# Multiplying the first MLP weight into attention's landmark values, batch by batch

## The chip, the cores and the metric

The kernel runs on one core of a Trainium2 chip. A core has TensorE (PE, matrix products), VectorE (DVE), ScalarE (ACT) and GpSimd (POOL), each with its own instruction stream that it executes in order, and SyncE (SP), whose queue starts most of the DMA transfers. The engines wait for each other by semaphores. Matrix products read SBUF and write PSUM. The metric is the device time of one execution in microseconds, as the median of several runs.

## The reference, cut to what matters

Nystrom attention over 8 batches of 8 heads, 576 rows of 64 elements each, with 32 landmarks a head, then a layer norm and a two-layer MLP with a residual:

```python
q_lm = q.reshape(B, H, 32, 18, D).mean(axis=3)      # landmarks; the same for k
A  = softmax(q @ k_lm.T / 8)                        # 576 x 32 for each head
Bm = softmax(q_lm @ k_lm.T / 8)                     # 32 x 32
C  = softmax(q_lm @ k.T / 8)                        # 32 x 576
Z  = Bm.T / (norm1(Bm) * norminf(Bm))
for _ in range(6):
    Z = 2 * Z - Z @ Bm @ Z
x  = A @ Z @ C @ v                                  # heads side by side: 576 x 512 a batch
xn = (x - mean(x)) / sqrt(var(x) + 1e-6) * g_ln
out = x + relu(xn @ w_ch1) @ w_ch2                  # 512 -> 2048 -> 512
```

For the change it matters that `x` of a batch is `A` (576 rows by 8 heads times 32 landmarks = 256) times `zc = Z C v`, and that the layer norm's division by a positive number a row can be done after the Relu and the second layer.

## The kernel before, in words

Work comes in units of four heads of one batch, two units a batch. Batches 0 and 1 go through `attention`, the others through `attention2` in the sets (2), (3, 4), (5, 6) and (7). For a set, a `Coming` object holds three queues of preparation: loads on SP's queue, casts to fp16 on POOL, and jobs. A job turns a tile with DVE's 32x32 transposes (`turn`), adds up segments of 18 rows for the landmarks (`add_up`; q's of most units are added on POOL), or spreads the sums with a small matmul into `psl` (`spread`), which ACT copies to `lm`. Then the set computes landmark scores (`psb`), scores of the landmarks of q with k (`psec`), the gram matrix (`psse`), the product with v (`pscv`), six iterations (`psn`), in which the scores of q with k's landmarks are done as well (`psea`, exponentiated into `ea`), and `zc` (`pszc`), spread by head masks into the block-diagonal tiles `zcbd`. `rows_of` then makes blocks of 128 rows of `x`: two matmuls of `ea` with `zcbd` into `psy`. The tiles `zcbd` have columns of head ones, so that `psy` also holds the softmax sums; DVE takes their reciprocals (`rcpd`) and multiplies, with a running row sum for the mean.

The MLP works on groups of 512 rows of `x`, nine in all, across batches. Each block is squared with an accumulator on ACT for the variance, centred (`center`, mostly on POOL) into `xn`, and turned by DMA (groups 0 and 1 by PE through `psxt`). The first layer contracts the 512 columns: for each of 16 chunks of 128 hidden columns, four matmuls of 512 columns into `psh`, which ACT passes through Relu to `hT`. The second layer is, in groups 0 to 3, 16 matmuls of 512 columns for each block into `pso`; in groups 4 to 8 it is a product of two-by-two blocks with seven products in place of eight (`pspa`, `pspe`, `pspc`, 256 columns a matmul), for which DVE adds and subtracts halves of `hT` (`hmix`) and POOL prepares mixes of `w2`. DVE or the additions of the products then form the output, which SP stores.

The order of the work is written out by hand. `mlp` is a generator of matmuls. `fill(n)` takes n pieces of it and is called between the steps of the attention, with counts that are listed for each set in `steps`; `prepare` casts, loads and runs jobs of the next set at the same places. All engines follow the program's order (`keep`). PSUM has three pools: `ps1` with one buffer, `ps2` with two (attention's larger tiles), and `psM` with three, for `psh`, `pso` and the product tiles. Nearly every instruction is issued by a helper, so in the profile matmuls have line L75, transposes by PE L79, and the ordered instructions of DVE, ACT and POOL L69; groups are told apart by their tiles' names.

Of the kernel before, what the change touches and what calls it, by code (L numbers as in the profile page):

```python
# [20 lines left out]
def kernel(  # L21
# [23 lines left out]
    G_FAST = 4  # L45
    HK, HN = MCH // 2, DM // 2
# [12 lines left out]
    nat = ctx.enter_context(tc.tile_pool(name="nat", bufs=8))  # L59
# [29 lines left out]
    raw = {0: {}, 1: {}}  # L89

    def load_qk(b):
        for u in range(U):
            raw[b]["q", u] = load(q, b, u, nc.sync)
            raw[b]["k", u] = load(k, b, u, nc.sync)

    def load_v(b):
        for u in range(U):
            raw[b]["v", u] = load(v, b, u, nc.sync)

# [7 lines left out]
    def cast_qk(b, u, nm, engine):  # L109
        t = nat.tile([P, NJ, 2, D], FP16, name="nat", tag="nat")  # L110
        engine.tensor_copy(out=t[:].rearrange("p j r d -> p r j d"), in_=raw[b][nm, u][:])
        nat_tiles[b, nm, u] = t

    def cast_v(b):
        natv_of[b] = natv = natv_buf[b % NV]
        for u in range(U):
            pool.tensor_copy(out=natv[:, u, :, :, 0:D].rearrange("p j r d -> p r j d"),
                             in_=raw[b]["v", u][:])

    nat_tiles, natv_of = {}, {}  # L120
    load_qk(0)
    load_v(0)
    g_sb = wpool.tile([P, KCH], FP32, name="g_sb")
    g_rows = wpool.tile([KCH, P], FP32, name="g_rows")
    keep(nc.sync.dma_start(out=g_rows[:], in_=moe_g_ln.rearrange("(c p) -> c p", p=P)))
# [11 lines left out]

# [6 lines left out]

# [13 lines left out]

# [16 lines left out]
    nc.vector.memset(eps_ln[:], 1e-6)  # L175

# [8 lines left out]
    zcbd_buf = []  # L185
    for i in range(NZ):
        zcbd_buf.append(const.tile([P, 4 * (D + 1)], FP16, name=f"zcbd{i}"))

    def zc_of(i):
        return zcbd_buf[i][:, ds(4 if i % 2 == 0 else 0, 4 * D)].rearrange("p (h d) -> p h d", d=D)

    cast_v(0)
    bones = const.tile([P, 4, 32], FP16, name="bones")
    for u in range(U):
        for nm in ("q", "k"):
            cast_qk(0, u, nm, dve)
        if u == 0:

            dve.tensor_copy(out=bones[:], in_=mask4[:, :, None].broadcast_to([P, 4, 32]))
            for i, t in enumerate(zcbd_buf):
                dve.tensor_copy(out=t[:, ds(0 if i % 2 == 0 else 4 * D, 4)],
                                in_=(mask4[:] if i < 2 else heads_of[i % 2]))


    load_qk(1)
    for u in range(U):
        for nm in ("q", "k"):
            cast_qk(1, u, nm, pool)  # L210
# [5 lines left out]
    xpool = ctx.enter_context(tc.tile_pool(name="xpool", bufs=15))  # L216

    def w_stage(src):
        stg = stage.tile([P, 2, DM], FP32, name="wstg", tag="stg")
        keep(nc.sync.dma_start(out=stg[:], in_=src))  # L220
        return stg

    def fetch_w1():
        coming = []
        for i in range(10):
            if i < 8:
                f, half = divmod(i, 2)
                coming.append(w_stage(w1_src[:, 2 * half:2 * half + 2, ts(f, DM)]))
            if i >= 2:
                f, half = divmod(i - 2, 2)  # L230
                stg = coming.pop(0)
                for c in range(2):
                    k = 2 * half + c
                    pool.tensor_scalar(out=w1_16[:, k, ts(f, DM)], in0=stg[:, c, :],
                                       scalar1=g_sb[:, k:k + 1], scalar2=0.0,
                                       op0=ALU.mult, op1=ALU.add)

    def fetch_w2():
        coming = []
        for i in range(12):  # L240
            if i < 8:
                coming.append(w_stage(w2_src[:, ts(i, 2), :]))
            if i >= 4:
                pool.tensor_copy(out=w2_16[:, ts(i - 4, 2), :], in_=coming.pop(0)[:])

    aprep = ctx.enter_context(tc.tile_pool(name="aprep", bufs=5))
    aexp = ctx.enter_context(tc.tile_pool(name="aexp", bufs=12))
    asm = ctx.enter_context(tc.tile_pool(name="asm", bufs=2))
    asum = ctx.enter_context(tc.tile_pool(name="asum", bufs=1))

    mstat = ctx.enter_context(tc.tile_pool(name="mstat", bufs=6))
    mxn = ctx.enter_context(tc.tile_pool(name="mxn", bufs=6))
    mxnT = ctx.enter_context(tc.tile_pool(name="mxnT", bufs=2))
    mhT = ctx.enter_context(tc.tile_pool(name="mhT", bufs=1))
    mout = ctx.enter_context(tc.tile_pool(name="mout", bufs=4))
# [4 lines left out]

# [13 lines left out]

    nat_pss, early_xT = {}, {}

    def sums(b, w, i, n16):
        for j in range(NJ):
            MM(nat_pss[b, i][:, w, :], n16[:, j, :, :].rearrange("p r d -> p (r d)"),
               pm16[:], start=(j == 0), stop=(j == NJ - 1), skip=True)  # L280

    def turn_part(w, nm, part):
        j0, j1 = ((0, 5), (5, NJ))[part]
        n16 = nat_tiles[1, nm, w]
        if part == 0:
            early_xT[1, nm, w] = aprep.tile([P, NJ, P], FP16, name="xT", tag="xT" + nm,
                                            bufs=5 if nm == "q" else 4)
        pst = psM.tile([P, 5, P], FP16, name="pst", tag="pm")
        for j in range(j0, j1):
            TR(pst[:, j - j0, :], n16[:, j, :, :].rearrange("p r d -> p (r d)"), ident16[:])  # L290
# [537 lines left out]
    def center(j, engine):  # L828
# [13 lines left out]
        if g < 2:  # L842
            return
# [435 lines left out]
```

The softmax here doesn't subtract the row's maximum and nothing guards it: scores larger than these inputs give would overflow.

## Time and profile before

| | us |
|---|---|
| time, median of three runs (lowest, highest) | 312.26 (311.87, 312.96) |
| span of the profiled execution, first to last instruction | 312.6 |
| PE busy | 303.4 |
| DVE busy | 191.6 |
| ACT busy | 155.6 |
| POOL busy | 140.7 |
| granted TensorE clock, mean | 0.989 |
| HBM read, written | 36.70 MB, 9.44 MB |

The profile is of one execution. It lists the busy time of each engine, the same in 40 equal slices of the span (a digit is tenths), groups of like instructions with their count, busy time and mean length, the idle time before them with what ended it, the chain of work that ended last, and the instructions in order of time. The profiler models the ends of matmuls, which are pipelined, so a busy PE need not be working at its full rate; how far apart matmuls start tells that.

### The profile page before, as it was taken

Reading aid. Unit: us, or ns where it says so; the run is one execution under the profiler, and the core shown is the slowest. Engines: PE = TensorE matmul, PEld = TensorE weight load, DVE = VectorE, ACT = ScalarE, POOL = GpSimd, SP = SyncE. Lnnn points to the kernel's source line nnn. Section 1 sums busy time; section 2 is a strip of 40 time slices with the busy share of each in tenths; the row PEclk is TensorE's granted clock in tenths of the full one; section 3 lists DMA queues with packets and bytes.
Section 4 is the critical chain, followed back from the end, with each engine's and each line's share of the span. In section 5 each row is a group of like instructions: output and inputs, shape, how many; then the busy total and the mean of one; then the engine's idle time right before and its main releaser. Section 6 shows DMA issues by size and latency. Waiting matters only on the chain.

```text
span 312.6 us, 8486 instructions
## 1 busy us (share of the span) xinstructions
PE 303.4 (97%) x3475; PEld 180.4 (58%) x3475; DVE 191.6 (61%) x525; ACT 155.6 (50%) x309; POOL 140.7 (45%) x191
## 2 busy tenths in 40 slices
PE   7899999999999999999999999999999999999994
PEld 7567764544444544544454468547844874685583
DVE  3648328957785326899256787749644980671364
ACT  2447783468524871277354761693147506405600
POOL 4479878974979595598097412030002240000000
PEclk9959999999999999999999999999999999999999
DMA  7999999999997877850159401540050516105013
GB/s 267 390 387 385 386 388 285 334 237 308 264 234 157 286 190 208 132 204 0 37 87 250 98 2 36 122 81 5 0 136 5 65 37 142 25 3 134 0 36 101
DMA packets 38863, 50.36 MB, mean 161 GB/s; under 512 B 17572, under 2 KB 18088, under 8 KB 38824
## 3 DMA queue, kind: packets, MB, share of 16 engines
q1 hardware_dynamic: 38504, 49.43, 56.4%
q8 instruction: 27, 0.44, 0.6%
q10 hardware_dynamic: 320, 0.39, 0.4%
q14 instruction: 12, 0.10, 0.1%
HBM read 36.70 MB, written 9.44 MB: 148 GB/s over the span
## 4 chain that ended last, share of the span: by engine, by line
PE 93%; DMA 2%; DVE 2%; issue 1%; SPq 0%; ACT 0%
PE psh L75 41%; PE pso L75 18%; PE pspa L75 8%; PE pspe L75 6%; PE pspc L75 6%; PE psy L75 3%; DMA stg<-in_k_dram 2%; PE psn L75 2%; PE pscv L75 2%; PE psec L75 1%; PE pst L79 1%; PE psea L75 1%; PE psse L75 1%; PE psa L75 1%; DVE xblk L69 1%; PE psxt L79 1%
## 5 line engine op out<-in xcount | busy, mean ns | idle before, releaser
L75 PE MATMUL psh<-xnT,w 128*128 128x512 f16 (+1 forms) x640 | 136.4, 359 | 0.7 <-issue 0.7
L69 ACT ACTIVATE hT<-psh 128x512 f16<-128x512 f32 x144 | 84.7, 598 | 71.8 <-PE psh L75 71.5
L75 PEld LDWEIGHTS <-w 128*128 128x128 f16 x640 | 58.8, 98 | 56.3 <-issue 4.8
L75 PEld LDWEIGHTS <-hT 128*128 128x128 f16 x656 | 62.8, 98 | 30.3 <-issue 1.1
L75 PE MATMUL pso<-w,hT 128*128 128x512 f16 x256 | 61.1, 380 | 0.0
L69 POOL TENSOR_SCALAR xn<-xblk,negm,rstd 128x512 f16<-128x512 f32 x20 | 16.8, 851 | 67.3 <-DVE negm L69 33.1
L69 ACT ACTIVATE junk<-xblk,negm 128x512 f16<-128x512 f32 x36 | 25.9, 720 | 18.9 <-POOL negm L69 11.6
L69 DVE SCALAR_TENSOR_TENSOR xblk<-psy,rcpd 128x512 f32<-128x512 f32 (+1 forms) x40 | 27.6, 691 | 1.8
L69 DVE SCALAR_TENSOR_TENSOR st<-st,psn 128x128 f16<-128x128 f16 (+2 forms) x36 | 11.4, 317 | 24.7 <-PE psn L75 24.3
L69 DVE TENSOR_TENSOR hmix<-hT 128x256 f16<-128x256 f16 (+2 forms) x20 | 8.9, 444 | 21.6 <-ACT hT L69 21.6
L69 POOL CAST nat<-stg 128x1152 f16<-128x1152 f32 x15 | 17.1, 1145 | 8.9 <-DMA stg<-in_q_dram 5.0
L69 DVE STREAM_TRANSPOSE xT<-nat 128x576 uint32<-128x576 uint32 x24 | 18.5, 769 | 0.0
L69 DVE TENSOR_REDUCE part<-xT 128x32 f16<-128x576 f16 x26 | 18.3, 744 | 0.1
L69 DVE RECIPROCAL rcpd<-psy 128x8 f32<-128x8 f32 (+1 forms) x40 | 8.1, 202 | 15.8 <-PE psy L75 15.5
L69 DVE SCALAR_TENSOR_TENSOR ot<-pso,rstd,xblk 128x512 f32<-128x512 f32 x16 | 12.0, 748 | 8.3 <-PE pso L75 8.3
L75 PEld LDWEIGHTS <-hmix 128*128 128x128 f16 x160 | 15.6, 98 | 1.9 <-issue 0.2
L69 DVE TENSOR_TENSOR xblk<-pspa,xblk 128x256 f32<-128x256 f32 x38 | 14.0, 418 | 4.2 <-PE pspa L75 4.2
L69 POOL CAST nat<-ring 128x1152 f16<-128x1152 f32 x12 | 13.6, 1144 | 6.7 <-DMA ring<-in_k_dram 3.3
L75 PE MATMUL psy<-zcbd,ea 128*128 128x260 f16 (+1 forms) x80 | 15.9, 284 | 0.0
L69 POOL CAST natv<-stg 128x1152 f16<-128x1152 f32 x10 | 11.4, 1161 | 7.6 <-DMA stg<-in_v_dram 7.6
L75 PEld LDWEIGHTS <-st 32*32 32x32 f16 x448 | 5.6, 90 | 14.8 <-issue 8.0
L69 POOL TENSOR_TENSOR asum<-asum 128x256 f32<-128x256 f32 (+1 forms) x22 | 13.1, 594 | 1.7
(130 smaller groups left out, 382.7 us busy)
## 6 DMA issues: line engine op xcount, KB each, us to landing
wstg<-in_moe_w_ch_dram SPq DMA_DIRECT2D x16, 512.0 KB, 7.0
stg<-in_q_dram SPq DMA_DIRECT2D x10, 576.0 KB, 7.8
stg<-in_k_dram SPq DMA_DIRECT2D x10, 576.0 KB, 7.6
out_dram<-xblk SPq DMA_DIRECT2D x34, 128.0 KB, 2.3
out_dram<-ot SPq DMA_DIRECT2D x32, 128.0 KB, 2.7
stg<-in_v_dram SPq DMA_DIRECT2D x7, 576.0 KB, 9.5
ring<-in_k_dram SPq DMA_DIRECT2D x6, 576.0 KB, 6.4
ring<-in_q_dram SPq DMA_DIRECT2D x6, 576.0 KB, 6.1
```

The lines of the kernel that those rows point to most:

```text
L69: return lambda *args, **kw: keep(getattr(self.engine, op)(*args, **kw))
L75: keep(nc.tensor.matmul(o, l, r, start=start, stop=stop, tile_position=(rb, cb), skip_group_check=(skip or cb != 0)))
L79: keep(nc.tensor.matmul(o, i_, idn, is_transpose=True, tile_position=(0, 0)))
```

## The change

The first layer no longer contracts the 512 columns of a turned `xn`. For each batch, `zc` (turned, `pszt`, copied to `zt`) is multiplied into `W1`: eight matmuls of 64 rows by 32 columns, 512 wide, make 256 landmark rows times 512 hidden columns (`product_of_heads`, `psm`, copied to `m16` by ACT or DVE), four such groups for the 2048 hidden columns. The first layer is then `m16` times `ea`, two matmuls of 288 columns for each half of the 576 rows. For this q's softmax must be normalized in `ea` itself (`normalize`: sums by a matmul, `1/s` as Exp of minus Ln on ACT, a product on DVE for batches 0 and 1, on POOL else). The row mean falls away because the columns of `W1` (scaled by `g`) are centred: `less_mean` sums them with a matmul, `center_w1` subtracts in place on DVE; batch 0's product uses the uncentred `W1` and is corrected in `m16` with `rz`. Mean and variance come from DVE's `bn_stats` and `bn_aggr`. `psy` has no columns of ones and is copied to `xblk` as it is. Every fourth `psh` tile goes through Relu on DVE.

The MLP goes batch by batch: blocks that straddle two batches belong to the odd batch, whose `hT` starts with the 64 last rows of the batch before (copied by POOL). `mlp` interleaves the second layer of a batch with the first layer of the next. The second layer has no seven-product form; for batch 0 it goes by halves of the columns, as `W2` is loaded by halves. Batch 1 is a set of its own through `attention2`, with its product with v late (`late`). `W1` and `W2` are loaded earlier on SP's queue: `W1` before batch 1's q and k, `W2` before batch 1's v. No `xn`, no transposing DMAs, no mixes of `w2` or `h` remain.

```diff
+    def normalize(ea, engine):
+        pss = ps2.tile([P, 2, 512], FP32, name="psd", tag="p2")
+        for half in range(2):
+            MM(pss[:, half, 0:HS], ones_of_heads, ea[:, ts(half, HS)])
+        lns = alog.tile([P, 2, HS], FP32, name="lns", tag="lns")
+        act(lns[:], pss[:, :, 0:HS], AF.Ln)
+        act(lns[:], lns[:], AF.Exp, scale=-1.0)
+        engine.tensor_tensor(out=ea, in0=ea, in1=lns[:].rearrange("p a t -> p (a t)"), op=ALU.mult)
...
-                dve.reciprocal(
...
-                    in1=rcpd[rows, :, None].broadcast_to([n, 8, D]),
-                    op0=ALU.mult, op1=ALU.mult, accum_out=rowsum[j][rows, :])
+                dve.tensor_copy(out=xb[rows, :], in_=psy[rows, :])
...
+        dve.bn_stats(out=six[:], in_=x_blk[j][:])
+        dve.bn_aggr(out=stats_of[b][:, u, :], in_=six[:])
...
+    def less_mean(f):
+        psf = psM.tile([P, 512], FP32, name="psf", tag="pm")
+        for c in range(KCH):
+            MM(psf[:], lesser[:], w1_16[:, c, ts(f, 512)], start=(c == 0), stop=(c == KCH - 1))
+        scalar.copy(less(f), psf[:])
+    def center_w1(f):
+        dve.tensor_tensor(out=w1_16[:, :, ts(f, 512)], in0=w1_16[:, :, ts(f, 512)],
+                          in1=less(f)[:, None, :].broadcast_to([P, KCH, 512]), op=ALU.add)
...
+        def product_of_heads(f):
+            psm = ps2.tile([P, 2, 512], FP32, name="psm", tag="p2")
+            for r in range(2):
+                for e in range(2):
+                    for u in range(U):
+                        block = 2 * r + e if b == 0 else 2 * (e ^ u) + r
+                        rows = ds(64 * e, 64)
+                        MM(psm[ds(32 * block, 32), u, :], zt[rows, r, w0 + u, :],
+                           w1_16[rows, 2 * u + r, ts(f, 512)], rb=64 * e, cb=32 * block)
...
+            elif f % 2 == 0:
+                scalar.copy(t[:], psm[:])
+            else:
+                dve.tensor_copy(out=t[:], in_=psm[:])
...
-                    psh = psM.tile([P, 512], FP32, name="psh", tag="pm")
-                    for c in range(KCH):
-                        MM(psh[:], w1_16[:, c, ts(m, P)], xnT[:, c, :],
-                           start=(c == 0), stop=(c == KCH - 1))
-                    act(hT[:, m, :], psh[:], AF.Relu)
+            for half in range(2):
+                psh = psM.tile([P, HS], FP32, name="psh", tag="pm")
+                for u in range(U):
+                    MM(psh[:], m16[f][:, u, ts(m % 4, P)], ea[u][:, ts(half, HS)],
+                       start=(u == 0), stop=(u == U - 1))
+                o = hT[:, m, ds(base + HS * half, HS)]
+                if n % 4 == 3:
+                    dve.tensor_scalar(out=o, in0=psh[:], scalar1=0.0, scalar2=None, op0=ALU.max)
+                else:
+                    act(o, psh[:], AF.Relu)
...
-                if g >= G_FAST:
-                    yield from second_layer(g, hT, mixed)
...
+        for b in range(B):
+            ahead, done, owed = None, False, 0
+            for cols in second_layer(b):
+                yield cols
+                if ahead is None and b + 1 in ready:
+                    ahead = first_layer(b + 1)
+                owed += cols
+                if ahead and not done and owed >= 1024:
+                    owed -= 1024
+                    cols = next(ahead, None)
...
+    for i in range(8):
+        load_w1(i)
...
+    for _ in range(4):
+        b1.next_load()
+        b1.next_cast()
+    for i in range(8):
+        load_w2(i)
+        cast_w2(i)
...
+    sets = [Coming((1,), 1), Coming((2,)), Coming((3, 4), 1), Coming((5, 6)), Coming((7,))]
```

`fill` now counts matmul columns (512 for each piece asked for) in place of pieces, `lesser` is a tile of -1/512, `less` holds the negated column means, `ones_of_heads` has a block of ones for each head, and `UP` is a factor of 16 in `g` that the variance's scale takes out again.

## The prediction

> **What bounds the kernel now.** I read the page's busy shares and slices first, then the chain of work that ended last, then the groups by form, the busy time by stretch, and one piece of the timeline.
>
> ```profile
> PE 303.4 (97%) x3475; PEld 180.4 (58%) x3475; DVE 191.6 (61%) x525; ACT 155.6 (50%) x309; POOL 140.7 (45%) x191
> ...
> PE   7899999999999999999999999999999999999994
> ...
> DVE  3648328957785326899256787749644980671364
> ...
> PE 93%; DMA 2%; DVE 2%; issue 1%; SPq 0%; ACT 0%
> ```
>
> TensorE is busy from the second slice to the last and makes 93% of the chain; DVE, next, is at 61%, with single slices at nine tenths. Whether a busy PE is also a dense one, the chain in order of time tells (start, length, what):
>
> ```profile
> 254.61 1.75 PE pspc L75 x16
> 256.36 13.81 PE psh L75 x64
> 270.17 1.75 PE pspa L75 x16
> ```
>
> 64 matmuls of 512 columns take 13.81 us, 0.2158 each; 16 of 256 take 1.75, 0.109 each, each with weights of its own. So a column costs 0.417 ns and a matmul 2.5 ns more: 288 columns are 0.1225 us. Most of the span is this dense. The number of columns decides today.
>
> ```profile
> 37.91 0.36 PE psa L75 x8
> ...
> 63.84 0.52 PE psec L75 x26
> ...
> 219.77 1.31 PE pspa L75 x12
> 221.23 0.36 PE psea L75 x29
> ```
>
> Small matmuls in different places of the array run at once: psec is 32 matmuls of 288 columns (26 recorded), 3.9 us in a row, and takes 0.52. Entering such a group costs something: twelve 256-column matmuls are 1.31 us here, and psea begins only 1.46 us after them. From start to start such a group costs about 0.09 us beside its own work.
>
> The durations of the other engines come from the groups by form (busy us, mean ns of one | idle before):
>
> ```profile
> L69 ACT ACTIVATE hT<-psh 128x512 f16<-128x512 f32 x144 | 84.7, 598 | 71.8 <-PE psh L75 71.5
> ...
> L69 ACT ACTIVATE junk<-xblk,negm 128x512 f16<-128x512 f32 x36 | 25.9, 720 | 18.9 <-POOL negm L69 11.6 <-DVE negm L69 7.1
> ...
> L69 DVE SCALAR_TENSOR_TENSOR xblk<-psy,rcpd 128x512 f32<-128x512 f32 x32 | 22.1, 692 | 1.5
> ...
> L69 DVE STREAM_TRANSPOSE xT<-nat 128x576 uint32<-128x576 uint32 x24 | 18.5, 769 | 0.0
> ...
> L69 DVE TENSOR_REDUCE part<-xT 128x32 f16<-128x576 f16 x26 | 18.3, 744 | 0.1
> ...
> L69 DVE TENSOR_TENSOR zcbd<-pszc,heads 128x256 f16<-128x256 f32 x12 | 4.3, 419 | 4.0 <-PE pszc L75 4.0
> ...
> L69 DVE TENSOR_TENSOR hT<-hT 128x1024 f16<-128x1024 f16 x10 | 7.2, 722 | 0.0
> ...
> L69 DVE CAST nat<-stg 128x1152 f16<-128x1152 f32 x4 | 3.0, 760 | 5.4 <-DMA stg<-in_q_dram 4.0 <-DMA stg<-in_k_dram 1.4
> ...
> L69 DVE TENSOR_SCALAR xn<-xblk,negm 128x512 f16<-128x512 f32 x2 | 1.6, 792 | 0.1
> ```
>
> A piece of the timeline (start, length), and one stretch of 18 us with each engine's busy time, PE, its weight loads, DVE, ACT, POOL:
>
> ```profile
> 137.54 0.77 DVE L69 STREAM_TRANSPOSE xT<-nat 128x576 uint32<-128x576 uint32 x1
> ...
> 138.23 0.20 DVE L69 STREAM_TRANSPOSE sT<-s 128x64 uint32<-128x64 uint32 x1
> ```
>
> ```profile
> 122.00:140.00 18.00, 18.00 (x92) 8.72 (x92) 15.88 (x43) 7.71 (x18) 11.91 (x18) 1.00 0.79 193
> ```
>
> The two transposes start 0.69 us apart though the first lasts 0.77: a DVE instruction whose operands are there occupies DVE for its mean less about 0.08 us. The stretch has DVE at 15.88 of 18 us beside a PE at 100%: while rows of attention come out, DVE is nearly full already.
>
> **The change on PE.** All against the profiled execution, whose span of 312.6 us is 0.1% above the median of the runs, 312.26. First layer: 512 matmuls of 512 and 128 of 256 columns (124.4 us) become 512 of 288 (62.7): minus 61.7. Second layer: without the seven-product form, 256 of 512 and 560 of 256 columns (116.3) become 496 and 160 (124.5): plus 8.2. New are 32 groups of eight psm matmuls (zc times W1, 64 rows by 32 columns, 512 wide). Their nearest row is psa, the same tiles, 0.36 us for 512 and 64 columns in four places; with eight places one pass and the switch give 0.31, eight in a row would be 1.7, which psec's row speaks against. I take 0.42: 13.4. Column means of W1 (16 of 512): 3.5. Sums of q's softmax (32 of 288): 3.9. The transposed zc, at pszc's rate: 1.5. Batch 1 as a set and no turning of xn on PE (36 pst, 36 pss, 32 psxt, 36 psc out; 64 scores, 2 psl in): minus 5.3. Warm-up: plus 0.7. Together minus 35.8: 276.8 us, if nothing else binds.
>
> **The change on the other engines.** ACT: 192 Relus of 288 columns at about 0.41 (598 ns less 224 columns at 0.82), 16 pairs Ln and Exp of 576 (about 1.4 a pair), 14 copies of psm (1.0), against 36 squares with their read-outs (0.92 each), 144 Relus and the turned xn gone: near 158 against 155.6, no bound. POOL loses xn, W2's mixes and four W1 scalings, gains 12 products of ea (1.3): about 125. SP loses 28 transposing DMAs. W1 and W2 now stand on SP's queue before batch 1 (W1 before its q and k, W2 before its v). At the 385 to 390 GB/s of the early slices its v (15.5 MB into the queue) lands near 42 us; batch 0's two layers cover that, and its product with v comes late in its set. Two waits are new there. PE's column means of W1's first quarter stand between iterations 4 and 5 of batch 0, behind two loads that take the places of batch 1's q and k (cast at 14.4 and 16.5 us before); scaled, they are there at about 17.4, when PE stood at that iteration at 16.8: 0 to 1 us, with the rest of the iterations behind it. ACT's last W1 scaling waits for the eighth load, near 22.5 us, with the first Relus behind it: again under 1 us, inside the first stretch below, where another engine is longer, so I add nothing.
>
> DVE is the engine that gains work without losing as much. Lost: reciprocals, means and the mixes of h. Gained: 64 of the Relus (0.45 by the 256- and 512-column rows, 0.37 occupied), copies of psm (1024 columns, 1.15 occupied; for batch 0 eight 512-column ones at 0.61), 36 bn_stats with aggregates, four centrings of W1 (2048 halves, 1.1 occupied by the 1024 row's rate; 2.2 if it runs at the f32 rate). bn_stats has no row: 0.36 at the rate of the CAST above, 0.71 by the TENSOR_SCALAR on 512 f32, both occupied; I take 0.57, a cycle-per-element rate like the reduction's. Over all it is about 212 us occupied. That is less than PE's, so the mean hides it. But PE's order in the changed kernel has joints that DVE must reach first: zc (pszt), and psl, the matmul that spreads the next set's landmark sums. A PE that waits there has that set's scores (psb, psec) queued behind, whose Exp on ACT and transposes on DVE the gram waits for. Between joints, in us (PE at the rates above without switches; DVE occupied):
>
> - batch 0's zc to batch 1's gram: PE 14.6, DVE 28.7 (8 psm products, 8 Relus, 5 psy copies, 4 transposes, 6 reductions, 4 centrings, 4 bn_stats)
> - batch 1's zc to batch 2's psl: PE 12.9, DVE 19.2
> - batch 2's zc to the second psl of batches 3 and 4: PE 14.6, DVE 20.7
> - their zc to the second psl of 5 and 6: PE 25.5, DVE 35.7
> - all other stretches: PE above DVE, nearest 26.8 to 23.6
>
> Work behind DVE in its order is what PE needs: every fourth Relu stands behind psy copies, bn_stats and transposes, and PE's psh tiles have two banks to rotate in while pso holds the third. So the longer engine sets each stretch. The excess is 14.1 + 6.3 + 6.1 + 10.2, less about 3.3 for PE's own switches there (some 36 of 0.09): 33.4. Off that go 2 us that PE already loses early (9.42 of 10 in the stretch from 20 to 30 us) and 1.2 at each joint, since a filling of 1.7 us stands between the last sum and psl: 4.8. So 276.8 + 33.4 - 2 - 4.8 = 303.4 us.
>
> The Trainium skill, "VectorE: DVE Perf Modes", section "The DRAIN you can't avoid", says that the next op does not start until the pipe of the one before has emptied. The timeline above shows starts 0.08 us before the end of the record, so I count occupied times. Taken as forbidding all overlap, the rule would give rival (b)'s sum.
>
> **Rivals.** (a) DVE's excess hides: PE runs ahead and DVE makes up later. For it: DVE's total of 212 is far below the span, and at 88% it stopped nothing in the stretch shown. Against: then DVE evicted a tile once in 16 matmuls, now once in eight of psh, and psl cannot be passed. Price: 277 to 296. (b) Slower: DVE's instructions do not overlap, because each now waits for a fresh result of PE, ACT or POOL. The four stretches hold 211 of them; each 0.01 us is 2.1 us. At full means they take 33.2, 22.4, 24.1 and 41.5, 17 more: 320. It decides from 0.04 us an instruction, half the overlap, where the time passes 312. (c) Slower: psh's two banks bind where PE should. A tile takes 0.245 us to fill, 0.16 until the result is there (the 380 ns of a 512-column matmul's record less its 0.2158), 0.41 to evict, and two handovers: about 1.0 against two periods of 0.46 where one pso goes between; 137 tiles in the other stretches, 0.03 to 0.1 us each and longer behind a 1.0 us copy: 4 to 14 us, 307 to 318. (d) The product is not concurrent: 1.7 a group, plus 41 us; psec's row makes this very unlikely.
>
> **How the numbers follow.** Forecast, 296 to 311: 0.45. (a) 0.20. Within 0.3% of 312.3, which is about what a measurement can tell: 0.04. (b) 0.18, (c) 0.12, (d) 0.01. Faster 0.65, same 0.04, slower 0.31. The unknown bn_stats moves the sum by 4.6 down or 3 up, the centring by 4.3 up; both lie inside. The range for eight in ten takes most of (a), (b) and (c): 283 to 321; the forecast's own is 296 to 311.
>
> **What would show it.** PE busy time falls by some 30 to 40 us of work, but windows between zc and psl show DVE near 95% and PE waiting for hT, m or psl released by DVE; the stretches after psl are PE-dense. psh x64 no longer appears; psh pairs cost 0.245. Wrong would be: PE dense throughout and a time near 277 (a), DVE's rows back to back yet longer than I took (b), or PE waiting for ACT's hT outside those stretches (c).

## The result and the profile after

The changed kernel takes 374.61 us (372.60 to 378.27 over four runs) against 312.23: 1.195 times as long (95% interval 1.188 to 1.202). The forecast was 303.4 us, with 283 to 321 as its range: wrong in sign and size. The execution profiled took 378.27 us, 1.0% above the median; its span is 376.6.

The page of the changed kernel, the lines that answer to those shown of before (busy time by engine, slices, granted clock, the chain by engine):

```profile
PE 301.1 (80%) x3476; PEld 158.6 (42%) x3476; DVE 226.0 (60%) x479; ACT 148.6 (39%) x311; POOL 122.9 (33%) x154
...
PE   7667747786599768787967699978987969989996
...
DVE  3346998348966697433889566745785613683221
...
PEclk9895995889999898998989799999999998999999
...
PE 49%; DVE 25%; ACT 9%; issue 6%; DMA 5%; POOL 3%; SPq 1%; DVEq 0%; POOLq 0%; ACTq 0%
```

No engine is full: PE went from 97% to 80% of the span, DVE is at 60, ACT at 39. TensorE's share of the chain fell from 93% to 49%. PE's busy time is nearly what it was (303.4 to 301.1) although its matmuls have fewer columns. The Trainium skill, "Perfetto Trace Analysis", section "Identifying the Most-Contended Engine", says that matmul busy time is not a good measure of how close a kernel is to its limit, as matmuls are pipelined, and advises, beside the share of peak operations, the busy time of the weight loads; here these went from 180.4 (58%) to 158.6 (42%).

What PE waited for, in the view of waits of PE alone (us in total, times, longest). Before, the whole list holds seven single waits, led by these two:

```profile
PE idle L75 <- DVE zeros L130: 1.6, 1, 1.6
PE psh L75 <- issue: 0.7, 1, 0.7
```

After, the first eight of 25 lines:

```profile
PE psh L75 <- ACT hT L69: 19.3, 30, 2.9
PE psh L75 <- DVE hT L69: 7.4, 8, 1.8
PE psh L75 <- ACT m L69: 6.6, 6, 3.1
PE psh L75 <- DVE xblk L69: 4.8, 7, 1.5
PE psm L75 <- DVE zt L69: 4.5, 5, 2.5
PE psn L75 <- DVE st L69: 3.8, 3, 2.7
PE psg L79 <- DMA g_rows<-in_moe_g_ln_dram: 3.1, 1, 3.1
PE psd L75 <- ACT lns L69: 3.0, 2, 2.6
```

Counting gaps of over 30 ns between matmul records, PE waited 12 times for 5.0 us in all before, and 110 times for 71.7 us after; 40.3 us of that, in 74 places, were before a `psh`. A wait costs more than its gap: `psh` matmuls of a dense run start 0.1225 us apart, but the last one ahead of a wait is recorded with its full 0.29 us, which nothing overlaps. Taking each record ahead of a gap less the usual spacing of its shape, that is 18.2 us more (1.8 before).

The busy time by stretch (start:end, length, PE, its weight loads, DVE, ACT, POOL, then granted clock, DMA share, GB/s). The first four lines are the four stretches in which the forecast saw DVE as the bound; the last four are stretches where PE was to be dense:

```profile
26.20:62.50 36.30, 23.54 (x188) 10.21 (x188) 29.52 (x52) 15.82 (x37) 17.52 (x18) 0.79 0.77 246
...
80.10:104.40 24.30, 15.81 (x148) 9.87 (x148) 19.99 (x41) 9.52 (x22) 4.62 (x4) 1.00 0.52 148
...
123.10:150.40 27.30, 20.45 (x137) 9.46 (x137) 21.26 (x43) 10.20 (x23) 21.41 (x26) 0.87 0.55 156
...
176.40:222.20 45.80, 34.08 (x232) 16.07 (x231) 37.64 (x73) 17.14 (x39) 19.83 (x22) 0.89 0.36 96
...
62.50:80.10 17.60, 14.90 (x237) 10.08 (x238) 7.34 (x22) 3.86 (x6) 11.70 (x13) 0.75 0.10 25
...
222.20:257.10 34.90, 31.06 (x566) 16.16 (x566) 19.32 (x44) 19.33 (x38) 11.58 (x12) 1.00 0.35 85
257.10:292.70 35.60, 29.76 (x233) 15.21 (x232) 25.02 (x48) 14.08 (x33) 0.76 (x1) 1.00 0.15 36
292.70:376.60 83.90, 73.98 (x643) 38.49 (x642) 34.28 (x71) 27.15 (x60) 3.60 (x3) 0.97 0.19 45
```

In the four stretches DVE is busy 108.4 us, close to the 104.3 that the forecast counted. But they last 133.7: DVE is busy 81% of them, and so neither engine is the bound. Outside them PE is busy 207.2 us in 242.9.

How they come to wait in turn is seen in a piece of the timeline (start, length, engine, operation; in brackets the engine's idle time before it and who ended it), from the stretch that follows the zc of batches 5 and 6:

```profile
260.54 0.41 PE L75 MATMUL psm<-w,zt 64*32 64x512 f16 x8
...
261.02 1.23 DVE L69 CAST m<-psm 128x1024 f16<-128x1024 f32 x1 [1.79 <-PE psm L75]
...
261.54 0.42 PE L75 MATMUL psh<-ea,m 128*128 128x288 f16 x2
...
262.28 0.69 DVE L69 COPY xblk<-psy 64x512 f32<-64x512 f32 x1
...
263.01 0.69 DVE L69 BATCH_NORM_STATS2 six<-xblk 128x6 f32<-128x512 f32 x1
263.38 0.38 PE L75 MATMUL pso<-w,hT 128*128 128x512 f16 x1 [0.50 <-ACT hT L69]
263.74 0.18 DVE L69 BATCH_NORM_AGGREGATE stats<-six 128x2 f32<-128x6 f32 x1
263.95 0.46 DVE L69 TENSOR_SCALAR hT<-psh 128x288 f16<-128x288 f32 x1
...
264.46 0.40 PE L75 MATMUL psh<-ea,m 128*128 128x288 f16 x2 [0.71 <-DVE hT L69]
```

DVE first waits 1.79 us for PE's `psm`. Then it copies it (1.23), and in its order copies rows and takes their statistics, and only at 263.95 passes on a `psh` tile that PE had filled by 262.42. With that bank and the one of a finished `pso` not yet read, PE soon runs out of banks and stands 0.50 and 0.71 us here, in a stretch in which DVE is busy for 70% of the time.

Three theories were put against each other. **D**: DVE's load in the stretches after zc. **N**: the normalization, whose sum, Ln, Exp and product stand in the order of PE, ACT and DVE or POOL ahead of what PE needs. **E**: the two banks of `psh`, with evictions too slow or too late.

### The profile page after: what moved, and what is told of

Read it like the earlier page. It is cut to its first block, busy times and chain, and to the rows that moved or that the text cites. A ratio compares the mean times of both kernels' runs of the same rounds, so it can differ in the third digit from the quotient of the medians.

```text
span 376.6 us, 8343 instructions
## 1 busy us (share of the span) xinstructions
PE 301.1 (80%) x3476; PEld 158.6 (42%) x3476; DVE 226.0 (60%) x479; ACT 148.6 (39%) x311; POOL 122.9 (33%) x154
## 4 chain that ended last, share of the span: by engine, by line
PE 49%; DVE 25%; ACT 9%; issue 6%; DMA 5%; POOL 3%; SPq 1%; DVEq 0%; POOLq 0%; ACTq 0%
PE pso L75 24%; PE psh L75 11%; DVE xblk L69 5%; DVE m L69 4%; DVE part L69 4%; DVE six L69 4%; PE psm L75 3%; DVE xT L69 3%; DMA g_rows<-in_moe_g_ln_dram 2%; ACT lns L69 2%; ACT hT L69 2%; POOL ea L69 2%; DVE hT L69 2%; DMA stg<-in_k_dram 2%; ACT m L69 2%
## 5 line engine op out<-in xcount | busy, mean ns | idle before, releaser
L75 PE MATMUL pso<-w,hT 128*128 128x512 f16 (+1 forms) x656 | 178.2, 370 | 2.8 <-ACT hT L69 2.8
L75 PE MATMUL psh<-ea,m 128*128 128x288 f16 x512 | 106.4, 298 | 40.3 <-ACT hT L69 19.3
L69 ACT ACTIVATE hT<-psh 128x288 f16<-128x288 f32 x192 | 76.8, 411 | 97.9 <-PE psh L75 97.3
L75 PEld LDWEIGHTS <-m 128*128 128x128 f16 x512 | 49.8, 101 | 96.8 <-issue 57.1
L69 DVE TENSOR_SCALAR hT<-psh 128x288 f16<-128x288 f32 x64 | 28.4, 444 | 31.2 <-PE psh L75 30.9
L69 DVE SCALAR_TENSOR_TENSOR xblk<-pso,rstd,xblk 128x512 f32<-128x512 f32 (+1 forms) x41 | 27.8, 678 | 26.4 <-PE pso L75 26.4
L69 DVE COPY xblk<-psy 128x512 f32<-128x512 f32 (+1 forms) x40 | 27.2, 680 | 10.4 <-PE psy L75 10.1
L69 DVE CAST m<-psm 128x1024 f16<-128x1024 f32 x14 | 17.1, 1222 | 19.5 <-PE psm L75 19.5
L69 DVE BATCH_NORM_STATS2 six<-xblk 128x6 f32<-128x512 f32 x36 | 25.0, 694 | 1.2
L69 DVE TENSOR_REDUCE part<-xT 128x32 f16<-128x576 f16 x32 | 22.4, 742 | 0.0
L75 PE MATMUL psy<-zcbd,ea 128*128 128x256 f16 (+1 forms) x80 | 16.2, 286 | 1.4 <-DVE m L69 0.9
```

Source lines behind the costliest of these rows:

```text
L69: return lambda *args, **kw: keep(getattr(self.engine, op)(*args, **kw))
L75: keep(nc.tensor.matmul(o, l, r, start=start, stop=stop, tile_position=(rb, cb), skip_group_check=(skip or cb != 0)))
```

## The experiments

All are edits of the changed kernel (374.6 us), and each time is the median of four runs. "..." stands for parts of an edit that are not shown. The runs of one kernel spread over 2 to 10 us, so a difference of some 3 us is not told apart.

**No normalization.** `normalize` does nothing:

```diff
     def normalize(ea, engine):
-        pss = ps2.tile([P, 2, 512], FP32, name="psd", tag="p2")
...
+        pass
```

> The normalization of q's softmax is left out (no sums psd, no Ln, Exp and no product on ea; the output is not normalized). Against 374.6 us of the changed kernel. Theory N (the normalization's chain of psd, Ln, Exp, product stands in the order of ACT, DVE and POOL ahead of what PE needs; the chain that ended last has 7.9 us of lns, 10.9 of ea and 1.9 of psd on it, and ACT waited 11.0 us more for POOL's products): 345 to 355. Theory D (DVE's load between the joints sets the time): only four products on DVE (4.2 us) and 3.9 us of matmuls go, 368 to 371. Theory E (the two banks of psh and their evictions in order set it): ACT loses 21 us of Ln and Exp, of which a part stood before Relus, 362 to 370.

354.67 us (353.41 to 357.48), 19.9 less: as N had it, and more than its 3.9 us of matmuls and 4.2 of DVE. From gram to zc the stretches shrink by 4.6 (batch 1), 0.5, 4.9, 3.4 and 5.1 us. The timeline of the changed kernel in batch 1's iterations shows why:

```profile
68.28 0.66 PE L75 MATMUL psd<-ea,bones 128*128 128x288 f16 x4
...
68.74 0.65 ACT L69 ACTIVATE lns<-psd 128x576 f32<-128x576 f32 x1 [1.32 <-PE psd L75]
...
69.42 0.68 ACT L69 ACTIVATE lns<-lns 128x576 f32<-128x576 f32 x1
69.97 0.24 PE L75 MATMUL psn<-st 32*32 32x64 f16 x8
...
70.14 0.78 DVE L69 TENSOR_TENSOR ea<-ea,lns 128x576 f16<-128x576 f16 x1 [1.44 <-ACT lns L69]
71.01 0.65 ACT L69 ACTIVATE lns<-psd 128x576 f32<-128x576 f32 x1 [0.90 <-DVE ea L69]
71.69 0.68 ACT L69 ACTIVATE lns<-lns 128x576 f32<-128x576 f32 x1
72.41 1.02 DVE L69 TENSOR_TENSOR ea<-ea,lns 128x576 f16<-128x576 f16 x1 [1.49 <-ACT lns L69]
...
73.75 0.27 DVE L69 SCALAR_TENSOR_TENSOR st<-st,psn 128x128 f16<-128x128 f16 x1
74.07 0.24 PE L75 MATMUL psn<-st 32*32 32x64 f16 x8 [2.67 <-DVE st L69]
```

PE's `psn` of 69.97 is ready at 70.2, but the iteration's `st` stands on DVE behind two products. The second Ln waits 0.90 us for the first product, as there is one tile `lns`, and DVE is idle for 1.49 us meanwhile. PE waits 2.67 us.

**All Relus on ACT.**

```diff
-                if n % 4 == 3:
+                if False:
                     dve.tensor_scalar(out=o, in0=psh[:], scalar1=0.0, scalar2=None, op0=ALU.max)
```

> All 192 Relus on ACT in place of every fourth on DVE. DVE loses 64 x 0.36 = 23 us, ACT gains 64 x 0.41 = 26 us. Theory D: about half of the 64 stand in the four stretches where DVE is longer than PE, so 360 to 365. Theory E: the evictions of one engine queue behind each other and behind Exps and copies on ACT, 374 to 385. Theory N: 372 to 378, as ACT's waits stay.

363.64 us (361.60 to 366.34), 11.0 less, as D had it, though ACT gets all 64 more (its busy time goes from 148.6 to 171.3 us).

**Statistics from 32 columns.**

```diff
-        dve.bn_stats(out=six[:], in_=x_blk[j][:])
+        dve.bn_stats(out=six[:], in_=x_blk[j][:, 0:32])
```

> The variance is taken from 32 of 512 columns (bn_stats on 32 columns; the rest of the statistics is left out). DVE loses 36 x 0.6 = 21 us, nearly all in the stretches after zc, where rows come out; nothing else changes. Theory D: 353 to 358. Theory E: DVE's own Relus and pso outputs come sooner behind shorter work, PE waited 7.4 and 4.8 us for those, 366 to 372. Theory N: 372 to 376.

361.92 us (360.61 to 362.72), 12.7 less: D's direction, at two thirds of its price. An instruction goes from 0.694 to 0.194 us, so 18 us of DVE's time gave 12.7.

**Short Relus on ACT.**

```diff
...
-                    act(o, psh[:], AF.Relu)
+                    act(o[:, 0:32], psh[:, 0:32], AF.Relu)
```

> ACT's 144 Relus... that is, three of four, pass 32 of 288 columns only (hT lies in two fixed tiles filled with zeros at the start; most of the hidden layer is left out). Each lasts about 0.2 in place of 0.41 us. Theory E: PE's waits of 19.3 us for ACT's hT halve or better, and ACT is sooner at the copies of psm and lm: 352 to 362. Theory D: DVE's work is as before, 370 to 375. Theory N: ACT's wait for POOL's products stays, 368 to 374.

374.74 us (371.73 to 376.73); the start is 3.6 us later (the first `psb` at 19.3 in place of 15.7 us) for the two zero fillings, so at most some 4 us were gained. E in its plain form, evictions that last too long on ACT, falls.

**Normalization through PSUM, three fp16 buffers.**

```diff
-    alog = ctx.enter_context(tc.tile_pool(name="alog", bufs=1))
+    alog = ctx.enter_context(tc.tile_pool(name="alog", bufs=3))
...
-        lns = alog.tile([P, 2, HS], FP32, name="lns", tag="lns")
-        act(lns[:], pss[:, :, 0:HS], AF.Ln)
-        act(lns[:], lns[:], AF.Exp, scale=-1.0)
+        act(pss[:, :, 0:HS], pss[:, :, 0:HS], AF.Ln)
+        lns = alog.tile([P, 2, HS], FP16, name="lns", tag="lns")
+        act(lns[:], pss[:, :, 0:HS], AF.Exp, scale=-1.0)
```

> The normalization stays whole, but Ln is taken in place in PSUM, and 1/s comes out in fp16 with three buffers in place of one of fp32. ACT then no longer waits for POOL's product before the next Ln (11.0 us of waits in the profile), and the products may be shorter. Leaving the normalization out gave 354.7 us. If the single buffer makes most of its price: 357 to 364. If it is the length of the chain psd, Ln, Exp, product in front of the iterations and of the first layer: 368 to 374.

364.35 us (362.40 to 365.74), 10.3 less: half of N's price. The groups by form, the product on DVE of the changed kernel, then of this one:

```profile
L69 DVE TENSOR_TENSOR ea<-ea,lns 128x576 f16<-128x576 f16 x4 | 4.2, 1050 | 5.6 <-ACT lns L69 5.6
```

```profile
L69 DVE TENSOR_TENSOR ea<-ea,lns 128x576 f16<-128x576 f16 x4 | 2.3, 575 | 3.9 <-ACT lns L69 3.9
```

The buffer, the operand and the place of Ln's result changed together; ACT's 11.0 us of waits for POOL's products are gone, the four products on DVE save 1.9 us, and POOL's twelve take the same as before (1.28). So most of the 10.3 is put down to the buffer, with the time just above the range expected of it; no run separates the three.

**Relus to ACT, copies of psm to DVE.**

```diff
-            elif f % 2 == 0:
-                scalar.copy(t[:], psm[:])
             else:
                 dve.tensor_copy(out=t[:], in_=psm[:])
...
```

> All Relus on ACT, and all 28 copies of psm to m on DVE (14 more, 1.14 us each). DVE loses 23 us of Relus and gains 16 of copies. If DVE's load as such sets the time, it is worth a third of the 11 us that moving the Relus alone gave: 369 to 373. If it is the order on DVE (a Relu that PE's next psh bank waits for stands behind a copy of psm, a psy copy and bn_stats, 2.6 to 3.2 us), 356 to 365, at or below the run with the Relus alone moved (363.6), as ACT's copies no longer stand before Relus either.

375.23 us (372.23 to 377.25): both expectations miss. The 11 us of the Relus are gone again, though DVE has less to do than in the changed kernel. This line of PE's waits tells where:

```profile
PE psh L75 <- DVE m L69: 11.5, 9, 3.0
```

In the changed kernel PE's waits for `m` from DVE before a `psh` were 0.7 us. So neither the load as a sum nor the place of the Relus alone is the price. What fits is that something PE needs next, a Relu or an `m`, is queued on DVE behind rows. The granted clock was lower as well (0.909 to 0.922 in the four runs, 0.930 to 0.940 in those of the changed kernel), and no run tells the two apart.

**Idle matmuls against the falling clock.** After each filling up to the end of batch 1:

```diff
...
             fill(count)
+            if c is sets[0]:
+                warm(1, 384)
...
```

> An idle matmul of 384 columns after each filling up to the end of batch 1 (about 30, 4.8 us of PE work), to see whether the clock that falls to 0.64 and 0.72 between 30 and 80 us costs time of its own. If it does: clock over 0.9 there and 366 to 371. If the slow clock only stretches matmuls in stretches where PE waits anyway: the same or up to 4 us more, 374 to 379.

380.05 us (375.78 to 385.71), not better, and above both ranges. In the execution profiled, the longest of the four, the clock of the same two stretches (by time) hardly rose, to 0.81 from 0.79 and 0.75:

```profile
26.20:62.50 36.30, 26.82 (x201) 11.48 (x199) 27.80 (x50) 16.28 (x38) 18.44 (x18) 0.81 0.81 249
62.50:80.10 17.60, 13.39 (x219) 8.73 (x220) 8.70 (x22) 4.19 (x8) 11.71 (x13) 0.81 0.08 20
```

So this edit does not tell what a full clock would be worth; the idle matmuls stood in the same order behind the same waits and could not fill them. But the four runs differ among themselves: the shortest had a mean clock of 0.948, the longest 0.910.

**All Relus and psy copies on ACT.**

```diff
-                dve.tensor_copy(out=xb[rows, :], in_=psy[rows, :])
+                scalar.copy(xb[rows, :], psy[rows, :])
...
```

> All Relus and all 40 psy copies on ACT. DVE loses 23 and 25 us, ACT gains 26 and about 24. Theory D, load on DVE: the four stretches lose about 20 us more than with the Relus alone, of which PE's own work lets half through, 350 to 356. Theory E, evictions in order: Relus now stand behind psy copies on ACT, 363 to 370, no better than the Relus alone moved (363.6).

355.86 us (352.72 to 359.41), 7.8 less than with the Relus alone: D again, at a third of the 25 us moved.

**Both causes together** (the previous edit and the fp16 normalization).

> All Relus and psy copies on ACT, and the normalization through PSUM with three fp16 buffers. Alone these gave 355.9 (Relus and copies) and 364.4 (normalization) against 374.6. If the two causes are separate stalls, their gains add up, 18.7 and 10.2: 343 to 349. If they are the same stalls (ACT blocked before a Relu): 352 to 357.

339.05 us (337.15 to 342.30): 35.6 less, more than the sum of 18.7 and 10.3, and below the range expected of separate stalls. They are not the same stalls; why the gains more than add up is not shown. The mean clock rose with them, to 0.952 to 0.968 from 0.926 to 0.957 in the runs of the two edits alone.

**hT's 64 rows copied by DVE.**

```diff
-            pool.tensor_copy(out=hTs[b + 1][:, :, 0:64], in_=hT[:, :, S - 64:S])
+            dve.tensor_copy(out=hTs[b + 1][:, :, 0:64], in_=hT[:, :, S - 64:S])
```

> Only the copy of 64 rows of hT moved from POOL to DVE, four instructions of 1.0 us on POOL, about 0.7 on DVE. In POOL's order they waited 46.0 us with the casts of the next set behind them; the chain that ended last has 11.0 us of loads of k and v on it that start late. If POOL's blocked casts cost time: 363 to 370. If they have slack: 373 to 378.

374.75 us (374.08 to 379.44): POOL's blocked casts have slack.

**The combination with POOL freed**: that copy and all products on DVE, and `g`'s load first in SP's queue.

```diff
+    keep(nc.sync.dma_start(out=g_rows[:], in_=moe_g_ln.rearrange("(c p) -> c p", p=P)))
...
         raw["q", u] = load(q, 0, u, nc.sync)
...
-                    normalize(ea[2 * (it - W // 2) + w], dve if late else pool)
+                    normalize(ea[2 * (it - W // 2) + w], dve)
...
```

> The combination with POOL freed: hT's copy and all products of the normalization on DVE (0.58 us each in fp16, in place of 1.28 on POOL), and the small load of g first in SP's queue. Against the combination: if POOL's order (products behind casts and sums, casts behind the copy of hT) is the next stall, and g's wait of 3.1 us at the start is on the path: 8 to 14 us less. If PE's two banks and ACT's evictions hold what is left: 0 to 4 us less.

340.96 us (339.83 to 342.00), 1.9 more than the combination, where both expectations had less. The start gains 1.8 us (first zc at 22.4 in place of 24.2), and it is lost again later. POOL is not the next stall.

**The combination with short Relus** (32 columns, all on ACT).

> The combination, with every Relu on 32 of 288 columns (hT in fixed tiles filled with zeros at the start, which costs about 4 us there; most of the hidden layer is left out). ACT loses 256 x 0.2 = 51 us. If psh's two banks and ACT's evictions hold the rest of the excess: 15 to 25 us less than the combination. If it is the joints (zc, psl, the normalization) and what stands in order ahead of them: 0 to 8 us less.

337.50 us (334.73 to 338.94): 1.6 less, or some 7 if the late start (first zc 5.9 us later) is taken off. ACT has 49 us less to do, and the time hardly moves. Throughput of evictions is not what is left.

**The first layer spread evenly**, alone and on the combination. In the changed kernel the account of owed columns runs from the start of a batch's second layer, so that the tiles stand one to one with single second-layer matmuls as soon as zc is there:

```diff
+            left = DM * MCH * (4 + b % 2)
...
                     ahead = first_layer(b + 1)
+                    owed, share = 0, left // 36
                 owed += cols
-                if ahead and not done and owed >= 1024:
-                    owed -= 1024
+                left -= cols
+                if ahead and not done and owed >= share:
+                    owed -= share
```

> The changed kernel with one edit: the first layer's tiles of a batch are spread evenly over what is left of the second layer of the batch before. In the trace they stand one to one with single second-layer matmuls after zc (a period of 0.46 us on PE, while rows, copies of psm and a Relu are all to be done by ACT and DVE in it), and the iterations then have only second-layer matmuls. If this bunching makes the stretches after zc too dense for DVE and ACT: 355 to 366. If the load per stretch counts as it did in the forecast, whatever its order: 372 to 377.

> The combination (339.1) with the first layer spread evenly. If bunching holds what is left: 322 to 331. If with ACT and DVE relieved there is slack enough: 336 to 341.

371.46 us (368.63 to 374.22) and 335.76 (331.12 to 339.99): about 3 us each, at the edge of what four runs tell apart; the first lies just under the range of no effect, the second just under that of slack. Bunching is a small part at most.

**Each copy of psm in two halves**, ACT and DVE side by side, on the combination, and with the even spread.

```diff
...
-            elif f % 2 == 0:
-                scalar.copy(t[:], psm[:])
             else:
-                dve.tensor_copy(out=t[:], in_=psm[:])
+                scalar.copy(t[:, 0, :], psm[:, 0, :])
+                dve.tensor_copy(out=t[:, 1, :], in_=psm[:, 1, :])
```

> The combination (339.1) with each copy of psm split into a half on ACT and a half on DVE (about 0.6 us each, side by side, in place of 1.02 or 1.22). If PE's waits for m (6.5 us before psh, 8.8 before the weights, and Relus behind the copy) count: 328 to 335. If the halves only wait for two engines' queues in place of one: 338 to 346.

> Both on the combination. If both count and are separate stalls, the sum of their gains: 314 to 327. If one covers the other: the lower of the two runs with one of them, within 3 us.

341.09 us (340.02 to 343.29) and 338.53 (336.12 to 341.46): no gain. A half is 0.59 us on ACT and 0.69 on DVE, and now each `m` waits for two queues.

**Row statistics later on ACT.** Of PE's waits before `psh` in the changed kernel, 10.1 us in four places ended with a Relu (in one place a copy of `psm`) that stood on ACT behind `lnv` and `rstd`, the Ln and Exp for 1/std of a batch's rows. From the waits of all engines:

```profile
ACT lnv L69 <- DVE stats L69: 24.3, 8, 5.2
```

ACT stands there until DVE has done the batch's last aggregate, and nothing needs the result before the second layer's first output. The edit issues them in the ninth matmul of that layer:

```diff
+        if u == 3 + b % 2:
+            stats_done.add(b)
+
+    def rstd_of(b):
         n = 4 + b % 2
-        if u == n - 1:
+        if b in stats_done and b not in rstds:
             lnv = mstat.tile([P, 5], FP32, name="lnv", tag="lnv")
...
+                    if m == 8:
+                        rstd_of(b)
...
```

> The changed kernel with one edit: ACT's Ln and Exp for 1/std of a batch's rows are issued when the second layer of that batch is under way, in place of right after its last block's statistics. ACT waited 24.3 us there for DVE's last aggregate, and of PE's waits before psh 10.1 us ended with a Relu behind them, in four places. If this is a stall of its own: 358 to 366. If PE only meets the next stall (DVE's Relu, which stands behind the same statistics on DVE): 371 to 375.

> The combination (Relus and psy copies on ACT, normalization through PSUM with three fp16 buffers), the even spread (335.8 together), and the late Ln and Exp of the row statistics. In the combination 11.4 us of PE's waits ended behind those two instructions, and no Relu is left on DVE. A stall of its own: 321 to 328. Otherwise 333 to 337.

369.53 us (367.26 to 373.45) alone, 5.1 less: between the two expectations, and its longest run overlaps the changed kernel's shortest (372.60). With the combination and the even spread 329.11 (326.45 to 330.21), 6.7 less than without: no overlap there, and again between the two expectations. Its page and PE's waits:

```profile
PE 283.6 (87%) x3476; PEld 154.0 (47%) x3476; DVE 176.2 (54%) x375; ACT 187.6 (57%) x415; POOL 123.7 (38%) x154
```

```profile
PE psh L75 <- ACT hT L69: 7.4, 16, 1.2
PE psl L75 <- DVE part L69: 4.4, 4, 1.3
PE psh L75 <- ACT m L69: 4.2, 7, 0.8
PE psse L75 <- DVE st L69: 3.7, 1, 3.7
```

That is 45.5 of the 62.4 us that the change lost, and still 5.1% slower than the kernel before (interval 4.6 to 5.7%). PE's gaps are down from 71.7 to 40.4 us and come from many places; no line of the list is over 8 us. A kernel faster than the one before was not found.

## Why the prediction was wrong

**PE's work: right.** `psm` was the unknown; a group of eight takes 0.343 us start to start at full clock, 0.42 taken. A `psh` matmul is 0.1225 us in a dense run, as forecast. That PE is busy 207.2 us outside the four stretches, where the forecast gave 205.9, is chance, as this time holds full records ahead of waits and matmuls at half clock. A fairer count takes from each profiled span the gaps, the full records ahead of them and what half clock cost PE (21.9 us after, 3.1 before, see below): 376.6 - 71.7 - 18.2 - 21.9 = 264.8 us, against 312.6 - 5.0 - 1.8 - 3.1 = 302.7: 37.9 less, forecast 35.8. For the 2 us that the forecast takes off as PE's early loss, the row it names (9.42 of 10) shows 0.6, beside a clock of 0.85.

**DVE's work: nearly right.** `bn_stats` is 0.694 us, 0.57 taken, 0.71 the upper bound; centring 1.22, and 1.14 from start to start, 1.1 taken. The overlap of 0.08 us holds for independent instructions only. A copy of `psy`, the statistics that read it and the aggregate that reads those start 0.72 and 0.73 us apart in the chain, a little more than their full length: 1.44 us where the forecast's terms, 0.61 (0.69 less 0.08) and 0.57, give 1.18. Rival (b) was right in effect for these, 9 us over 36 blocks, though not in its reason: they wait for DVE's own result, not for another engine. So far the rule holds that the prediction quotes from the Trainium skill, "VectorE: DVE Perf Modes", section "The DRAIN you can't avoid"; the section adds that an instruction that is not held starts earlier, and independent ones do so here (xT 0.69 us apart at 0.77 each). The measured busy 108.4 in the four stretches against 104.3 shows that the sum was not the fault.

**"So the longer engine sets each stretch": this step failed.** It took the time of a stretch as the maximum of two sums. With in-order engines and tiles handed over one by one the time here lies above it: the four stretches, with DVE busy 108.4 us and PE 93.9, lasted 133.7 us where the forecast gave them 97.5 (DVE's 104.3 less the 6.8 it took off): 36.2 more. The runs put it down to DVE's order, in which a Relu, an `m` or an `st` that PE needs stands behind row copies and statistics: taken away one by one, Relus gave 11.0 us, psy copies 7.8 and statistics 12.7, parts of which are the same stalls. Where they gave it can be measured between the same tiles of each profiled execution (from `pszt` to the `psse` or `psl` that ends the stretch; one execution each, for the changed kernel the longest of its four):

| us | four stretches | the rest |
|---|---|---|
| forecast | 97.5 | 205.9 |
| changed kernel | 133.7 | 242.9 |
| Relus on ACT | 122.8 | 240.4 |
| Relus and psy copies on ACT | 110.3 | 247.4 |
| short statistics | 118.1 | 240.8 |
| no normalization | 128.4 | 223.0 |
| fp16 normalization, three buffers | 128.2 | 232.5 |
| best version | 102.7 | 225.1 |

**"If nothing else binds": this failed too, by as much.** The rest of the span was given 205.9 us and took 242.9, 37.0 more. The normalization was costed by its instructions alone, with no wait: leaving it out takes 19.9 us off the kernel, in the profiled executions 19.9 of 25.2 us outside the four stretches, for its latency on three engines and its single buffer. The step "where you add a wait, what is queued behind it" was done for W1's loads and not for this, nor for `lnv` on ACT (5.1) and for `g`, for which PE waits 3.1 us at the start since its turn was moved ahead of the iterations. The waits for W1 were as small as forecast: the matmuls of its column means waited for nothing but, once, 0.3 us for a bank.

**The clock had no term of its own.** All rates of the forecast are those of full clock. In the profile of the changed kernel the clock was at half for 51.2 us, in which PE was busy 43.8 (before: 6.8 and 6.2). At half clock `psh` matmuls start 0.24 us apart in place of 0.12, so half of that, 21.9 us, went to the clock on PE, 3.1 before. This is inside the two excesses above, not beside them, and it is an upper bound, as PE might only have waited more. What points to a real price: in each of the 19 kernels of four runs here the longer runs tend to have the lower clock, by 2.3 us for each 0.01 if all are taken together. For the 0.059 between the two profiles that would be some 14 us, an estimate from a correlation; no edit moved the clock alone.

**Rival (c)** named the right banks but a wrong mechanism: a period of 1.0 against 0.92. Its price was 4 to 14 us outside the four stretches; PE's waits before `psh` there are 13.4 us in 26 places, inside that range by luck, and twice as much, 26.9 us in 48 places, lies inside the stretches. Shortening ACT's Relus, which that sum would have rewarded, gave next to nothing; the eviction starts late, which counts for more than how long it is. Rival (a) is refuted: PE's lead is two tiles of `psh`, 0.9 us with one `pso` matmul between each (0.245 and 0.216), and the pieces of 1 to 3 us that stand on the other engines are longer.

**What stays open**: the 16.6 us by which the best version is behind the kernel before (against the forecast its profile is 5.2 over in the four stretches and 19.2 over in the rest), the price of the clock by itself, and whether a third bank for `psh` would have made the order harmless, which was not tried.

## What to carry to other kernels

A maximum over engines' sums is a floor for a stretch, not its forecast (here 108 us of DVE became 134): list for each instruction that the bound engine waits for what stands ahead of it in its engine's order, and compare that time with the cover that the free buffers give. A chain that is added over three engines can cost its latency where the next step stands behind it in program order (19.9 us here); give it buffers and a place after what is needed first. Replacing long matmuls by short ones takes cover away: the same late Relu that before had tiles of 0.86 us in front of it now has tiles of 0.245. No run varied this by itself.

## What the runs showed of the hardware

TensorE's clock fell without a long gap. Stretches of the changed kernel, columns as above (the clock is the third number from the end): twice the 3.4 us ahead of a fall, and the fall:

```profile
54.30:57.71 3.41, 1.40 (x54) 0.73 (x51) 2.55 (x6) 1.93 (x7) 0.00 (x0) 1.00 0.00 0
57.71:67.95 10.24, 7.76 (x90) 4.27 (x78) 7.30 (x16) 3.24 (x6) 4.00 (x4) 0.50 0.01 2
...
122.56:125.97 3.41, 1.73 (x29) 0.65 (x28) 2.38 (x7) 1.01 (x1) 3.25 (x5) 1.00 0.92 277
125.97:129.39 3.42, 3.42 (x19) 1.35 (x19) 0.94 (x1) 0.82 (x2) 3.26 (x4) 0.50 1.03 284
```

The longest gap of PE was 2.0 us (at 54.4) ahead of the first of these falls and 0.9 us (at 123.5) ahead of the second; PE was idle for 2.0 and 1.7 us of the 3.4. Then the clock is at half while PE is busy, in the second all the time. The group of eight `psm` at 29.4 us, at half clock too, takes 1.10 us. Over the span the clock is 0.93, 0.989 before. It is higher in some versions that wait less (0.956 without the normalization, 0.968 and 0.972 in the combinations), but not with the Relus, or the Relus and psy copies, on ACT (0.927 and 0.926). The Trainium skill, "TensorE: Matmul & The Clock Gate", section "HAM oscillation — how this bites in real kernels", gives gaps of over about 3.4 us as what to avoid; here the clock was halved after shorter ones. Its section "A second HAM failure mode: psum-queue depth-cycling", on frequent short idling between groups, is nearer to what is seen here.

The same DVE product of 576 elements took between 0.76 and 1.65 us in the changed kernel (fp32 reciprocals), and on average 0.575, 0.609 and 0.852 in three versions with fp16 ones (the normalization alone, the combination, the split copies), while POOL's took 1.27 to 1.28 in all. What makes the spread on DVE was not tested.
